# First key and query loads regrouped by queue, first packed queries transposed by halves, one last store, one widening step on GpSimd, and another order

## The chip, the cores and the metric

The kernel runs on one core of a Trainium2 chip. Its time is the device time of one execution in microseconds; the number compared is the median of the runs shown. An engine executes its own instructions in the order in which they were recorded, and waits for other engines and for transfers through semaphores. TensorE is called PE, VectorE DVE, ScalarE ACT, GpSimd POOL and SyncE SP. SP computes nothing here; it issues almost all transfers.

## The reference

Two blocks follow each other: attention through 32 packed queries for each head, then a gated feed-forward block with a convolution of three taps.

```python
# q, k, v: (8, 8, 576, 64) float32, p: (8, 8, 32, 64) float32
def sm_attn(qq, kk, vv):
    s = scale * np.matmul(qq, kk.transpose(0, 1, 3, 2))
    s = s - np.max(s, axis=-1, keepdims=True)
    a = np.exp(s)
    a = a / (np.sum(a, axis=-1, keepdims=True) + 1e-09)
    return np.matmul(a, vv)
p_packed = sm_attn(p, k, v)
out = sm_attn(q, p_packed, p_packed)
x = out.transpose(0, 2, 1, 3).reshape(8, 576, 512)
# w_in (512, 1024), conv_w (3, 1024), w_out (1024, 512): float64
h = np.maximum(x @ w_in, 0.0)
conv_out = sum(conv_w[k] * shifted(h, k - 1) for k in range(3))
gate = 1.0 / (1.0 + np.exp(-conv_out))
return (h * gate @ w_out).astype(np.float32)
```

## The kernel before, in words

The 64 pairs of batch and head are worked through in 16 groups of four heads, `g` = 0 to 15; a batch `b` has two groups. For a group, keys and queries are loaded (`load_kq`) and transposed into `kT` and `qT`: for the first four groups on PE in two halves, five and four blocks of 128 columns (`half_transpose`, L684), which ACT or DVE copy out of PSUM; for the others on DVE (L644). The keys of group 0 come in two transfers of 640 and 512 columns (L606, L608), so that the first five blocks can be transposed ahead of the other four. `attention(g)` then makes the scores of the packed queries `pT` against the keys (L704), the maximum `nm` (L819, DVE), the exponential `a` with its sum (L823, ACT), its transpose (L835) and copy `a1T`, the product with the values (L843), the scaled result `pb` and its transpose `ppT` (L856 to L869), the scores against the queries (L704 again), their softmax on DVE, ACT and POOL (`s`, `mx`, L877 to L907), and the result split into a high and a low part, `a2hi` and `a2lo`.

The packed output is not formed: `packed_weight` multiplies `ppT` into `w_in` (L949, split by L977), and `ffn1(b, j)` (L1014, 12 matmuls for each of 64 pairs of batch and block of 128 columns) multiplies that with `a2`, in three products for the high and low parts. Relu, three taps and a tanh follow on ACT and DVE (L1029 to L1073; L1073 makes the finished block of `hgt`). `ffn2(m)` multiplies 36 tiles of 128 rows with `w_out`: two with plain float32 (L1142), the others with three products of parts (L1195). The last tile is made in two halves of 256 columns (`last_tile`, L1100).

The float64 weights come in as eight tiles of 1 MB. Each is turned to float32 on the core: the upper words by an ACT instruction (L441), the low words by another (`rounding`, L502), a shift on DVE (L445) and an addition on DVE or POOL.

Which engine does a movable step is written in the sets `ON_DVE` and `ON_POOL`. All steps are generators, and the string `ORDER` says in which order they are recorded, two characters for each step. `Flow` goes through it with a table of costs, and before the start of the second tile of `ffn2` it records idle matmuls on zeros (L287, called `warm`) wherever its table has PE waiting for at least one of them; seven matmuls on `stage` (L298) come ahead of everything.

SP issues `p` of the first four groups, queries, keys, values and weights in one fixed sequence. A transfer holds one of eight semaphores, so it waits for the transfer eight places ahead. The keys, queries and weights of the opening lie in `hgt` and `stage`, which are used again.

Of the kernel before, what the change touches and what calls it, by code (L numbers as in the profile page):

```python
# [26 lines left out]
    "140x3j3x3n3z145z0q3z5y5z3x5y3z5y1041143y0x410q0q3p3y3z5z3p7d413y3z0x42153n3p421e42433y443n3p43144238430x605y4344"
    "425y435z5z3p44191d1b1414600w420x5y1b446060435z43453l15421b143l443p45460x44601444456060464546146011464745601b6061"
    "460x45474645465z481b475y17600x0x136049484947611g0x491k141448494847474a4b1i484947184849484961616161621r1i38616162"
    "0x61611i611b381i624b621c0x620x6163141c1b62141n1b0x0x4b1i0x141a62621b6263621f1i14141j1b1p141j624a636363141i1i6363"  # L30
    "1p1p1b1b63646314141p4a1462631i1b391u1b4c4d4c4e4c644d1l1h391b1w1p4c4d4c4d1i634c651p1m641i644e1z1q4d1b644d1q1b1p4e"
    "4c1b1i1i641y1s1p4f641o1w4d1p4e64652164644g1w1i1i1w254f1t1b641x4f651i1x4g4f65644f232c1b4e4k1w4g1p1i4g4e4k4f4e4g1w"
    "65651w4g4k65651b1p1p63664g394h4i651i4f2d4h65664h4j4i231i4i1v65231w4j6666661w664j4h4i4h1p23284i2a23241w4j4h1i4l4l"
    "4j1i1w4j2a4h4j23664i4i66664l6665204m2a4n2a6767241w1p4m4o664n222f1w1p4n2a66674n67672b671p67264n674o4m4n4m67231p1p"
    "4m681w4n4m1p27231p674p234u1w4p2h234m681p674o2b2a4p4o681w2h4p694o684p692h682368292368684p4o4o4q1w23672h4p4q68684u"
    "4q682h1w4q2a4r4r69694s69236a2j4q4q4s4u4q69696a1w234t2a692a692m4r4s694s2o4r4v1w4t4r4t2k694r4s4t2i2a2h4t6a4r4s4s6a"
    "4t4t6a2a6a6a236b2i4v1w6a6a6a6b4w2e4v682o6a2h6b2a4w2o692h6b2g4x4w6b4w6b6b2l2q4x6c6a4y2a234x6b6b2p4x4w4w2o4y4x6b4x"
    "4w236c6b6d2a4x6d4z2x4z232a6c6c2t502h506c2a6c4y504y6c4z6c6c2r502o2a6c6c2p2h23544z2v4y2z2a2h2o4y6c6d6d6d4z236b4z2o"
    "2o6d4z2h506d546d2v6e4y2v2h2h6d6e6d546d5030516e2o50522s6f526e2v53516f2n6e2h2v6e6e2a526e2w532w5151536e6e5352322o51"
    "53522o6e552v536d516f2a2h526f2h512a6f53522h2o6g6f5556322v566f2o566f326f2h6f6g2o6f57586g2u57562o2v6g576g562y582h6g"  # L40
    "5632565759586h6h6e3259556g576g6g2v6g5959573257332v59582o6g595e5e335a6h2o6g59585e5a6h6h6h3258322h5b5a6i2o326h6h5a"
    "6f6h2o5a6i5a585b6h5b5b5a6h5c2o2v2v5b5d6j5b2v315d6i6i6j5d6i2v6i6i5d5c6i2v5d5c6i5d5c2v6i5d6i5f5c5c326j6j6j6j5c5b5f"
    "6j6j6k6i6k6j6j6l2o5f6j5g5h5g6l2v6k326k5g6k6k5i2v6k6k5g2v6k5h5g5g325i5g5i6k5h5h6j6k5j6m6l6l5i5h5i2v6l326l6m5i5j5h"
    "6l325h6l6h5j6l6l5i6l325k5k6m5k5j6n6m5j6m326l5j6m5l5k5j326m6m6m6m2v5m5k5l5k6n6m5l6n5k5n5l5m6m326n325m6n5l5m6n6n6o"
    "5l5n326n6n6o6n5n5o6n5o5m325p6o5p6o5l5m5n5o6o6o6o5n6o6o5p6o5n5n5m6n6p6o5q5r6p5r5q5q5s5r6p6p6p5q6o6p5q5r5q6q5q6p6p"
    "5r6q5s5r6p5s5t5r5s6p5u5t6p5t6q6r5t6q6q6p5s5t6q5u5t6r5u5t6k6q6q5u6q5v5u5s5s6q5u5w5u5v6q5w5x5v6r5x5v6r5x6r6s6s6r6r"
    "5x5w6r5w6r5v6r5x5w5v6s5x5w6s5v5w6s6s5x6s6r6s6t6s6s6r6t6u6t6t6t6t6t6u6t6s6t6q6t6u6t6u6u6u6v6v6u6u6t6u6u6v6u6v6v6w"
    "6s6v6v6v6v6u6v6v6w6w6w6w6x6w6w6w6w6w6x6x6x6v6x6x6x6x6x6w6x7e7e7e7e7e6x7e7e6x7e7e6w7e"
# [15 lines left out]
class Flow:  # L64
# [150 lines left out]
def tile_packed_attention_conv_gate(  # L215
# [1068 lines left out]
```

## Time and profile before

| | |
|---|---|
| median of three runs | 395.87 us (395.81 to 396.06) |
| the profiled execution | 396.32 us, of which the span is 394.5 us |
| PE busy | 386.9 us, 98% of the span |
| DVE, ACT, POOL busy | 336.0 us (85%), 246.1 us (62%), 77.8 us (20%) |
| transfers | 47.63 MB, mean 121 GB/s |

The span is what the profile shows, from the first to the last instruction. Busy shares are means over stages that differ: the transfers are dense in the first third and sparse after it. Matmuls are pipelined, so that neighbouring ones overlap in the profile; the pieces of the chain of waits give their distance instead.

### The profile page before, as it was taken

The numbers are of one execution on the slowest core, as the hardware profiler recorded it, in microseconds if no ns is written. First come the engines' busy times: TensorE is split into PE (matmuls) and PEld (weight loads), VectorE is DVE, ScalarE is ACT, GpSimd is POOL, SyncE is SP. The second block draws the span as 40 slices with busy tenths as digits, with TensorE's granted clock in tenths as the row PEclk, the third lists the DMA queues.
The fourth block names the chain that finished last, engine by engine and source line by source line (L and its number), as shares of the span: only waits on it lengthen the run. The fifth ranks groups of instructions, "written<-read, shape, count | busy, mean of one in ns | idle before, by whom it ended". The sixth has DMA issues, their size and how long they took to land.

```text
span 394.5 us, 8187 instructions
## 1 busy us (share of the span) xinstructions
PE 386.9 (98%) x3306; PEld 310.3 (79%) x3306; DVE 336.0 (85%) x503; ACT 246.1 (62%) x399; POOL 77.8 (20%) x58
## 2 busy tenths in 40 slices
PE   7999999999999999999999999999999999999996
PEld 6657665787778887979788797979798869898885
DVE  4899999999998999999998999899989797967110
ACT  3599999987667777866645545677454433544221
POOL 2042124104234443322002122101010022020020
PEclk9999999999999999999999999999999999999999
DMA  8998898995878995666393461010010000101111
GB/s 263 372 370 258 214 266 147 194 206 97 148 148 165 172 206 112 130 114 139 72 172 68 100 125 50 1 55 2 27 55 24 29 28 28 53 2 53 54 53 56
DMA packets 157543, 47.63 MB, mean 121 GB/s; under 512 B 145460, under 2 KB 148788, under 8 KB 157504
## 3 DMA queue, kind: packets, MB, share of 16 engines
q1 hardware_dynamic: 157104, 46.41, 50.0%
q10 hardware_dynamic: 368, 0.66, 0.6%
q8 instruction: 26, 0.43, 0.5%
q14 instruction: 13, 0.11, 0.1%
q0 software_dynamic: 32, 0.02, 0.0%
HBM read 37.64 MB, written 9.44 MB: 119 GB/s over the span
## 4 chain that ended last, share of the span: by engine, by line
PE 85%; DMA 5%; DVE 3%; ACT 3%; SPq 1%; issue 1%; DVEq 0%; ACTq 0%
PE fo L1195 41%; PE big L1014 23%; PE sm L1195 4%; DMA q<-in_q_dram 4%; PE big L1142 4%; PE big L704 4%; PE big L949 3%; PE sm L843 2%; PE big L835 2%; DMA hgt<-in_q_dram 2%; SPq L623 1%; PE fo L1100 1%; PE sm L1100 1%; PE big L684 1%; ACT hgt L1071 1%
## 5 line engine op out<-in xcount | busy, mean ns | idle before, releaser
L1195 PE MATMUL fo<-wo_hi,xhi 128*128 128x512 f32 x240 | 96.6, 402 | 0.0
L1195 PE MATMUL fo<-wo_lo,xhi 128*128 128x512 f32 x240 | 94.0, 392 | 0.0
L1195 PE MATMUL fo<-wo_hi,xlo 128*128 128x512 f32 x240 | 93.7, 390 | 0.0
L1071 ACT ACTIVATE hgt<-hgt 128x576 f32<-128x576 f32 x64 | 43.6, 688 | 28.8 <-DVE hgt L1067 28.7
L329 POOL TENSOR_TENSOR xlo<-hgt,xhi 128x1024 fp32r<-128x1024 f32 x14 | 35.7, 2548 | 130.4 <-DVE xhi L339 36.0
L1063 DVE SCALAR_TENSOR_TENSOR hgt<-hbuf,cw,hgt 128x576 f32<-128x576 f32 x64 | 53.4, 842 | 9.3 <-ACT hgt L1061 9.1
L1031 ACT ACTIVATE hbuf<-big 128x576 f32<-128x576 f32 x57 | 37.3, 655 | 30.2 <-PE big L1014 30.0
L1014 PE MATMUL big<-a2hi,ghi 128*128 128x288 f32 x256 | 55.8, 299 | 0.0
L1014 PE MATMUL big<-a2lo,ghi 128*128 128x288 f32 x256 | 54.6, 294 | 0.0
L1014 PE MATMUL big<-a2hi,glo 128*128 128x288 f32 x256 | 54.3, 293 | 0.0
L1195 PEld LDWEIGHTS fo<-wo_hi,xhi 128*128 128x128 f32 x240 | 45.1, 188 | 11.5 <-issue 2.2
L1195 PEld LDWEIGHTS fo<-wo_hi,xlo 128*128 128x128 f32 x240 | 45.1, 188 | 10.2
L1195 PEld LDWEIGHTS fo<-wo_lo,xhi 128*128 128x128 f32 x240 | 45.1, 188 | 7.3
L1067 DVE SCALAR_TENSOR_TENSOR hgt<-hbuf,cw,hgt 128x576 f32<-128x576 f32 x64 | 50.6, 808 | 0.2
L1073 DVE SCALAR_TENSOR_TENSOR hgt<-hgt,hbuf 128x576 f32<-128x576 f32 x64 | 48.4, 769 | 2.1 <-ACT hgt L1071 1.6
L1014 PEld LDWEIGHTS big<-a2hi,ghi 128*128 128x128 f32 x256 | 42.7, 188 | 5.5 <-issue 1.6
L1014 PEld LDWEIGHTS big<-a2hi,glo 128*128 128x128 f32 x256 | 40.9, 188 | 0.0
L1014 PEld LDWEIGHTS big<-a2lo,ghi 128*128 128x128 f32 x256 | 40.9, 188 | 0.0
L1210 ACT COPY o<-fo 128x512 f32<-128x512 f32 x30 | 17.6, 585 | 32.8 <-PE fo L1195 28.8
L1061 ACT ACTIVATE hgt<-hbuf,cw 128x576 f32<-128x576 f32 x47 | 36.2, 779 | 2.4 <-DVE hbuf L1029 1.7
L326 DVE TENSOR_TENSOR xlo<-hgt,xhi 128x1024 fp32r<-128x1024 f32 (+1 forms) x24 | 24.6, 1035 | 10.7 <-ACT xhi L341 10.5
L341 ACT CAST xhi<-hgt 128x1024 fp32r<-128x1024 f32 (+1 forms) x28 | 26.8, 957 | 8.8 <-DVE hgt L1073 4.5
(127 smaller groups left out, 576.5 us busy)
## 6 DMA issues: line engine op xcount, KB each, us to landing
out_dram<-o SPq DMA_DIRECT2D x35, 256.0 KB, 2.3
k<-in_k_dram SPq DMA_DIRECT2D x48, 144.0 KB, 3.3
q<-in_q_dram SPq DMA_DIRECT2D x48, 144.0 KB, 3.2
v<-in_v_dram SPq DMA_DIRECT2D x40, 128.0 KB, 3.2
v<-in_v_dram SPq DMA_DIRECT2D x6, 512.0 KB, 7.5
hgt<-in_moe_w_in_dram SPq DMA_DIRECT2D x3, 1024.0 KB, 12.5
hgt<-in_moe_w_out_dram SPq DMA_DIRECT2D x3, 1024.0 KB, 6.2
hgt<-in_q_dram SPq DMA_DIRECT2D x2, 576.0 KB, 6.9
```

The source lines that it names most:

```text
L326: nc.vector.tensor_tensor(**kw)
L329: added = nc.gpsimd.tensor_tensor(**kw)
L341: nc.scalar.copy(out=out, in_=in_)
L1014: nc.tensor.matmul(out=t[:, hf, :SH], lhsT=w[:, gg, js], rhs=x[:, hf * SH : (hf + 1) * SH], start=n == 0, stop=n == (1 if b in F1F else 3) ...
L1031: nc.scalar.activation(out=inner, in_=t[:, :, :SH], func=AF.Relu, scale=0.5)
L1061: nc.scalar.activation(out=d, in_=h[:, 1 : S + 1], func=AF.Copy, scale=cw[:, NJ + j : NJ + j + 1])
L1063: nc.vector.scalar_tensor_tensor(out=d, in0=h[:, 0:S], scalar=cw[:, j : j + 1], in1=d, op0=ALU.mult, op1=ALU.add)
L1067: nc.vector.scalar_tensor_tensor(out=d, in0=h[:, 2 : S + 2], scalar=cw[:, 2 * NJ + j : 2 * NJ + j + 1], in1=d, op0=ALU.mult, op1=ALU.add)
L1071: nc.scalar.activation(out=d, in_=d, func=AF.Tanh)
L1073: nc.vector.scalar_tensor_tensor(out=d, in0=d, scalar=1.0, in1=h[:, 1 : S + 1], op0=ALU.add, op1=ALU.mult)
L1195: nc.tensor.matmul(out=t, lhsT=x[:, c, :], rhs=w[:, c % 2, :], start=c + i == 0, stop=c == NJ - 1 and i == 2)
L1210: nc.scalar.copy(out=o, in_=t)
```

## The change

The first transfers are issued otherwise. On ACT's queue the first 640 columns of the keys of group 0, then its queries in one transfer, then the other 512 columns of the keys; before, the queries came from SP. The values of group 0 get a dependency on the first of these transfers. SP's sequence is another one, given by `ORDER`.

The first packed queries are transposed and scaled by halves: groups 0 and 1, then groups 2 and 3, each half with four transposes and one scaling.

The low words of the first weight tile (`r0`) may be multiplied on POOL, and are. In the opening four copies of `kT`, one of `a1T` and one of `a2hi` go from DVE to ACT and one of `qT` the other way (`kT15`, `kT20`, `kT25`, `kT35`, `a1T0`, `hi0`; `qT05`); more names change later. Costs in the table are changed, which moves idle matmuls: there are 27 instead of 31.

In the last half tile the copy out of PSUM is divided between ACT and DVE, and one store from SP takes the place of two stores of 64 rows from ACT and SP.

```diff
-    "36003602360300360403366y36016y346z34070405053a346z0a0a70340e090505083b700605060c3c050l0c05340h053b0h3e0c72053405"
+    "003603360236360036036y3604070504050a703a05340170053b0e0634340a060936760c080c363b6z3c050c050c050h050c05340l6z0h"
...
-    ON_DVE = {"a1T0", "hi0", "hi1", "hi12", "hi15", "kT10", "kT15", "kT20", "kT25", "kT35", "qT00", "relu35", "relu45", "relu61", "relu66", "relu67", "relu71", "relu74", "tap02", "tap36", "tap42", "tap43", "tap44", "tap46", "tap51", "tap52", "tap61", "tap63", "tap65", "tap66", "tap67", "tap70", "tap72", "tap73", "tap75", "x140", "x170", "x220", "x240", "x250", "x270", "x280", "x300", "x320"}
+    ON_DVE = {"gh510", "hi1", "hi12", "kT10", "qT00", "qT05", "relu34", "relu76", "tap00", "tap02", "tap40", "tap41", "tap42", "tap44", "tap46", "tap53", "tap56", "tap57", "tap60", "tap61", "tap64", "tap65", "tap67", "tap70", "tap72", "tap73", "tap74", "tap75", "tap77", "x140", "x180", "x230", "x270", "x280", "x310", "x340", "x90"}
...
+    def behind(added, old, reason):
+        info = mybir.DependencyInfo(mybir.DependencyClass.Sync, mybir.DependencyReason.DATA)
+        tc.add_manual_dep(added.ins, old.name, info, reason=reason)
...
-        if f"r{i}" in ON_DVE:
+        if key in ON_POOL:
+            old = [x for x in nc.cur_bb.bb.instructions if x.engine == mybir.EngineType.DVE][-2]
+            added = nc.gpsimd.tensor_scalar(out=r, in0=low, scalar1=2.0**-29, scalar2=None, op0=ALU.mult)
+            behind(added, old, "GpSimd waits for its turn beside VectorE")
+        elif key in ON_DVE:
...
+            if g == 0:
+                behind(first, keys[0].ins, "the first keys have the transfer engines to themselves")
...
-                nc.scalar.dma_start(out=t[:, :640], in_=rows[:, :640])
+                keys.append(nc.scalar.dma_start(out=t[:, :640], in_=rows[:, :640]))
...
+            if g == 0:
+                rows = src[b, :HG].rearrange("h (r s) d -> (h r) (s d)", r=NR)
+                nc.scalar.dma_start(out=t, in_=rows)
+                grp[g][name] = t
+                return
...
+            for gs in ((0, 1), (2, 3)):
+                for x in range(2):
+                    for db in range(2):
+                        first, r = x + db == 0, 64 * x + 32 * db
...
+                        nc.vector.transpose(
+                            out=pT[r : r + 32, 128 * gs[0] : 128 * gs[1] + 128].rearrange("d (h n) -> d h n", n=NP),
+                            in_=raw[:, HG * gs[0] : HG * gs[1] + HG, 32 * db : 32 * db + 32],
+                        )
+                yield Step("DVE", 202, two=True, sets=[("pT", g) for g in gs])
+                part = pT[:, 128 * gs[0] : 128 * gs[1] + 128]
+                nc.vector.tensor_scalar(out=part, in0=part, scalar1=SCALE, scalar2=None, op0=ALU.mult)
...
-        nc.scalar.copy(out=o, in_=t)
+        nc.scalar.copy(out=o[:, : DM // 4], in_=t[:, : DM // 4])
+        nc.vector.tensor_copy(out=o[:, DM // 4 :], in_=t[:, DM // 4 :])
         yield Step("SP", 600, give=["o"])
-        nc.scalar.dma_start(out=rows[:64, fs], in_=o[:64])
-        nc.sync.dma_start(out=rows[64:, fs], in_=o[64:])
+        nc.sync.dma_start(out=rows[:, fs], in_=o)
```

At the start of the program ACT issues two transfers before and three after, ahead of its first copies (in these names `hgt_75` is `hgt[0]`, where the first keys and queries lie, and `hgt_76` is `hgt[1]`). Before:

```order
L606 DMA hgt_75<-in_k_dram 128x640
L608 DMA hgt_75<-in_k_dram 128x512
L341 ACT_TABLE_LOAD
L341 COPY kT<-big 128x640
L341 COPY kT<-big 128x512
```

and with the change:

```order
L623 DMA hgt_75<-in_k_dram 128x640
L637 DMA hgt_75<-in_q_dram 128x1152
L625 DMA hgt_75<-in_k_dram 128x512
L345 ACT_TABLE_LOAD
L345 COPY kT<-big 128x640
L345 COPY kT<-big 128x512
```

The queries now stand between the two parts of the keys. SP's sequence at the same place was

```order
L760 DMA stage<-in_p_dram 32x16x64
L623 DMA hgt_75<-in_q_dram 128x1152
L586 DMA v_88<-in_v_dram 128x4x256
L595 DMA v_88<-in_v_dram 64x4x64
L623 DMA hgt_75<-in_k_dram 128x1152
L407 DMA hgt_76<-in_moe_w_in_dram 128x4x512
L623 DMA k<-in_k_dram 128x1152
```

and is now

```order
L783 DMA stage<-in_p_dram 32x16x64
L645 DMA hgt_75<-in_k_dram 128x1152
L411 DMA hgt_76<-in_moe_w_in_dram 128x4x512
L601 DMA v_88<-in_v_dram 128x4x256
L612 DMA v_88<-in_v_dram 64x4x64
L645 DMA k<-in_k_dram 128x1152
L645 DMA hgt_75<-in_q_dram 128x1152
```

The keys of group 1 and the first weight tile moved ahead of the values of group 0, and these two have nothing to wait for. On PE, just ahead of the first `ffn1` product (L1014 before), there stood, from the transposes of the queries of group 2 on,

```order
L684 MATMUL big<-ident,q 128x128 x5
L949 MATMUL big<-w_in_sb,ppT 32x256 x8
L684 MATMUL big<-ident,q 128x128 x4
L843 MATMUL sm<-v_88,a1T 32x64 x20
L835 MATMUL big<-ident,a_483 128x128 x5
L977 MATMUL big<-ghi,minus 128x256 x2
L866 MATMUL sm<-ident,pb 128x128
L287 MATMUL idle<-zeros 128x512 x2
L704 MATMUL big<-qT,ppT 32x288 x8
L287 MATMUL idle<-zeros 128x512
L1014 MATMUL big<-a2hi,ghi 128x288 x2
```

and now stands

```order
L706 MATMUL big<-ident,q 128x128 x5
L977 MATMUL big<-w_in_sb,ppT 32x256 x8
L726 MATMUL big<-kT,pT 32x288 x8
L292 MATMUL idle<-zeros 128x512 x2
L1005 MATMUL big<-ghi,minus 128x256 x2
L706 MATMUL big<-ident,q 128x128 x4
L292 MATMUL idle<-zeros 128x512 x2
L871 MATMUL sm<-v_88,a1T 32x64 x20
L1042 MATMUL big<-a2hi,ghi 128x288 x2
```

A transpose of `a`, a transpose of `pb` and a score against queries moved behind the first product. Of the idle matmuls 25 stood ahead of it and 6 behind; now it is 23 and 4.

## Rows read from the trace of the kernel before

**Rows 1.** Page, busy time, share and instructions by engine.

```profile
PE 386.9 (98%) x3306; PEld 310.3 (79%) x3306; DVE 336.0 (85%) x503; ACT 246.1 (62%) x399; POOL 77.8 (20%) x58
```

**Rows 2.** Windows: stretch, length, busy time by engine, granted clock, DMA share, GB/s.

```profile
0.00:5.00 5.00, 3.87 (x15) 3.42 (x16) 0.71 (x2) 1.28 (x1) 2.07 (x15) 1.00 0.64 186
5.00:10.00 5.00, 3.77 (x38) 2.68 (x38) 4.06 (x7) 2.16 (x5) 0.00 (x0) 1.00 1.06 345
...
46.40:105.00 58.60, 58.52 (x545) 40.93 (x546) 57.82 (x83) 51.88 (x82) 14.65 (x9) 1.00 0.88 174
...
390.60:394.50 3.90, 0.00 (x0) 0.00 (x0) 0.00 (x0) 0.37 (x1) 0.00 (x0) 0.95 0.14 36
```

**Rows 3.** Timeline of PE: start us, us, instruction, idle before it.

```profile
7.20 1.64 PE L684 MATMUL big<-ident,hgt 128*128 128x128 f32 x13 [1.23 <-DMA hgt<-in_q_dram]
...
9.08 0.72 PE L704 MATMUL big<-kT,pT 64*32 64x288 f32 x16
...
33.95 0.42 PE L1014 MATMUL big<-a2hi,ghi 128*128 128x288 f32 x2
...
40.91 1.56 PE L287 MATMUL idle<-zeros 128*128 128x512 f32 x6
...
46.38 0.72 PE L704 MATMUL big<-qT,ppT 64*32 64x288 f32 x16 [0.29 <-ACT ppT L869]
```

**Rows 4.** Transfers issued near 1.2 us: KB, us to landing.

```profile
hgt<-in_q_dram SPq DMA_DIRECT2D x1, 576.0 KB, 6.0
hgt<-in_k_dram ACTq DMA_DIRECT2D x1, 256.0 KB, 6.2
```

**Rows 5.** Transfer queues from 4.5 to 5.5 us: packets, MB, share of 16 engines.

```profile
q1 hardware_dynamic: 55, 0.24, 69.6%
q10 hardware_dynamic: 49, 0.10, 29.6%
```

**Rows 6.** Timeline of ACT and DVE in the opening.

```profile
8.45 0.59 ACT L341 COPY kT<-big 128x512 f32<-128x512 f32 x1 [1.97 <-PE big L684]
...
5.17 2.85 DVE L770 STREAM_TRANSPOSE pT<-stage 32x512 f32<-32x512 f32 x4 [3.58 <-DMA stage<-in_p_dram]
...
9.91 0.76 DVE L819 TENSOR_REDUCE nm<-big 128x1 f32<-128x576 f32 x1 [0.70 <-PE big L704]
11.77 0.82 DVE L339 COPY kT<-big 128x640 f32<-128x640 f32 x1 [1.11 <-PE big L684]
12.64 0.67 DVE L339 COPY kT<-big 128x512 f32<-128x512 f32 x1
...
32.60 0.75 DVE L326 TENSOR_TENSOR a2lo<-a2t,a2hi 128x576 fp32r<-128x576 f32 x1
```

**Rows 7.** Chain that ended last: start us, us, what; pieces for distances.

```profile
7.20 1.22 PE big L684 x9
32.57 0.46 PE idle L287 x2
54.66 0.65 PE big L704 x16
57.22 1.59 PE big L1014 x12
58.81 0.58 PE big L835 x5
```

**Rows 8.** A copy of 128 columns on ACT; the last copy and store; landings of stores.

```profile
16.39 0.26 ACT L869 COPY ppT<-sm 128x128 f32<-128x128 f32 x1
390.68 0.37 ACT L1113 COPY o<-fo 128x256 f32<-128x256 f32 x1 [2.50 <-PE fo L1100]
391.08 0.56 ACTq L1115 DMA_DIRECT2D out_dram<-o  x1
...
out_dram<-o SPq DMA_DIRECT2D x1, 128.0 KB, 1.7
out_dram<-o ACTq DMA_DIRECT2D x1, 64.0 KB, 2.4
```

More of the change, by code (lines that the diff above doesn't have):

```diff
@@ L27 @@
[L27 to L31, printed above, removed]
@@ L329, in tensor_tensor @@
         added = nc.gpsimd.tensor_tensor(**kw)
-        tc.add_manual_dep(
-            added.ins,
-            old.name,
-            mybir.DependencyInfo(mybir.DependencyClass.Sync, mybir.DependencyReason.DATA),
-            reason="GpSimd waits for its turn beside VectorE",
-        )
+        behind(added, old, "GpSimd waits for its turn beside VectorE")
     def copy(key, out, in_):
@@ L496, in rounding @@
     def rounding(i):
-        yield either(f"r{i}", 1048, 1135, two=True, after=[("we", i)], sets=[("wp", i)])
-        low, r = words.pop(i)
-        if f"r{i}" in ON_DVE:
+        key = f"r{i}"
+        on = "GP" if key in ON_POOL else "DVE" if key in ON_DVE else "ACT"
+        ns = dict(ACT=1048, DVE=1135, GP=R_GP)
+        opts = dict(ACT=(1048, False), DVE=(1135, True), GP=(R_GP, 0))
+        yield Step(
+            on, ns[on], either=(key, opts), two=on == "DVE", early=True, after=[("we", i)], sets=[("wp", i)]
+        )
+        low, r = words.pop(i)
+        if key in ON_POOL:
+            old = [x for x in nc.cur_bb.bb.instructions if x.engine == mybir.EngineType.DVE][-2]
+            added = nc.gpsimd.tensor_scalar(out=r, in0=low, scalar1=2.0**-29, scalar2=None, op0=ALU.mult)
+            behind(added, old, "GpSimd waits for its turn beside VectorE")
+        elif key in ON_DVE:
             nc.vector.tensor_scalar(out=r, in0=low, scalar1=2.0**-29, scalar2=None, op0=ALU.mult)
@@ L611, in load_kq @@
             yield Step(
-                "SP", 1450, after=after, late=500 * (g == 0), take=["kq"] * (g >= NG), sets=[(name, g)], parts=parts
+                "SP", 1450 + 450 * (name == "q" and g > 1), after=after, late=300 * (g == 0), take=["kq"] * (g >= NG), sets=[(name, g)], parts=parts
             )
@@ L757, in queries @@
         if i == 0:
-            yield Step("SP", 600, sets=[("p", 0)], late=1000)
+            yield Step("SP", 500, sets=[("p", 0)], late=1000)
             raw = stage[:NP, DFF:].rearrange("n (h d) -> n h d", d=D)
             nc.sync.dma_start(out=raw, in_=p[:2].rearrange("b h n d -> n (b h) d"))
-            plain = max([n + 1 for n in range(4) if n not in QUAD_K], default=1)
-            for x in range(2):
-                for db in range(2):
-                    yield Step(
-                        "DVE", 69 + plain * 133, after=[("p", 0)] * (x + db == 0), take=["pT"] * (x + db == 0), sets=[("pd", 0)] * (x + db == 2)
-                    )
-                    if x + db == 0:
-                        pT = wk.tile([128, 4 * HG * NP], F32, name="pT", tag="pT")
-                    r = 64 * x + 32 * db
-                    nc.vector.transpose(
-                        out=pT[r : r + 32, : plain * 128].rearrange("d (h n) -> d h n", n=NP),
-                        in_=raw[:, : HG * plain, 32 * db : 32 * db + 32],
-                    )
@@ L774, in queries @@
[L774 to L779 removed]
+            pT = None
+            for gs in ((0, 1), (2, 3)):
+                for x in range(2):
+                    for db in range(2):
+                        first, r = x + db == 0, 64 * x + 32 * db
+                        yield Step(
+                            "DVE",
+                            335,
+                            after=[("p", 0)] * first,
+                            take=["pT"] * (first and not gs[0]),
+                            sets=[("pd", 0)] * (x + db == 2 and gs[0] > 0),
+                        )
+                        if pT is None:
+                            pT = wk.tile([128, 4 * HG * NP], F32, name="pT", tag="pT")
+                        nc.vector.transpose(
+                            out=pT[r : r + 32, 128 * gs[0] : 128 * gs[1] + 128].rearrange("d (h n) -> d h n", n=NP),
+                            in_=raw[:, HG * gs[0] : HG * gs[1] + HG, 32 * db : 32 * db + 32],
+                        )
+                yield Step("DVE", 202, two=True, sets=[("pT", g) for g in gs])
+                part = pT[:, 128 * gs[0] : 128 * gs[1] + 128]
+                nc.vector.tensor_scalar(out=part, in0=part, scalar1=SCALE, scalar2=None, op0=ALU.mult)
+                for n in gs:
+                    grp[n]["pT"] = pT[:, 128 * n : 128 * n + 128]
```

76 lines of the change are left out of this document (42 added, 34 removed).

## The prediction

> **What bounds the kernel now.** I read the page's busy times first: PE is busy for 98% of the span, DVE for 85% [rows 1]. Then the windows. From 46.4 to 105 us PE is busy for 58.5 of 58.6 us, and the chain of waits runs on through PE to 390.6 us with no wait of it above 0.3 us. So the middle can hardly give time, only lose some. What is left is the opening, up to 46.4 us, and the 3.9 us behind the last matmul [rows 2]. In the same window DVE is busy for 57.8 of 58.6 us: a second engine stands close behind PE. Third, the timeline of PE in the opening: it waits 1.23 us at 7.20 for keys and queries, has its first score at 9.08, its first product of the feed-forward block at 33.95, and still runs six idle matmuls at 40.91; the score at 46.38 is the last piece that waits noticeably [rows 3]. From 5 to 10 us the transfers move 345 GB/s at a DMA share of 1.06: the opening waits for bytes first, and for DVE and ACT after that [rows 2].
>
> **The opening: bytes.** Before, the second part of the first keys was alone behind the first part on ACT's queue, landing at 7.4 (1.20 + 6.2); the queries, on SP's, at 7.2 (1.20 + 6.0) [rows 4]. Now the queries (0.59 MB) stand ahead of it on ACT's queue, while the keys of group 1 (0.59 MB) and the first weights (1.05 MB) are issued on SP's with nothing to wait for. The new dependency holds back only the values, which come third. How are two queues served together? From 4.5 to 5.5 us, 55 packets of SP's queue (q1) and 49 of ACT's (q10) moved, 0.24 and 0.10 MB: turns about even, and bytes by the size of the packets [rows 5]. Queries and keys of group 1 have rows of one size, and so have the second keys and the weights (2 KB), so I share bytes evenly. Up to the end of the second keys, then, 0.13 (packed queries) + 0.33 + 0.59 + 0.59 + 0.26 + 0.26 (weights) = 2.16 MB must move. By 5 us 0.93 MB are through (186 GB/s), the other 1.23 MB take 3.6 us at 345 GB/s [rows 2], and landings stood about 0.5 us behind such a sum: 9.2 us (an estimate). Its ends are 7.4, as now, if ACT's queue were served first, and 9.8.
>
> The Trainium skill speaks against the change here: the page "DMA: Bandwidth & Descriptors", section "Issuing engines are not separate DMA queues", says that DMAs of SP and ACT run on the same 16 engines and interleave. By it an order within ACT's queue keeps nothing away from what SP has issued, which is the 9.2 of the sum; the plain reading of the change, keys and queries one after the other undisturbed, would give about 7.2.
>
> **The first scores.** At 9.2 PE does the four blocks (about 0.5 us, of the 1.22 us for nine, [rows 7]), ACT copies them (0.59 us, [rows 6]), then comes an idle matmul (0.23 us, [rows 7]) and the score (0.65 us): first score at 10.6, first maximum on DVE at about 11.3 instead of 9.91 [rows 6]. Halving the transposes lets `pT` be ready some 1.6 us earlier (four at 0.71 us become four at about half, [rows 6]). That cover is worthless while the keys are late: DVE then stands idle from about 6.9 to 10.4 us.
>
> **DVE up to the second pair of parts.** The first product needs `a2lo` of group 1. From the first maximum to its end DVE takes 23.4 us now (9.91 to 33.35), of which 1.1 and 0.2 us idle; the 1.11 stands ahead of the copy at 11.77 [rows 6]. In the new order this stretch has three copies of `kT` of 512 columns (about 0.6 us each by their starts), one of 640, one of `a1T` (0.75 each) and one maximum (0.67) less; one copy of `qT` (0.6) and the second half of the packed queries (four at 0.36 and a scaling of 0.24) more [rows 6]. A shift and a high part less and a subtraction more give another 0.3 less. Net about 2.0 us less. The waits: the 1.1 us for the exponential again, and some 0.6 us where scores now come late. 11.3 + 23.4 - 1.3 - 2.0 + 1.7 = 33.1, against 33.35. With the bounds of the landing, 31.3 to 33.8.
>
> What left DVE costs ACT: four copies more and one widening step less (`r0`, on POOL now). For that step on POOL the trace has no row; two-operand instructions of 512 and 1024 columns there take 1.2 to 2.6 us. It must be done by the addition of the first weights, some 3 us after it can start, so I cost it at nothing; without that cover it would be up to 1.5 us late for DVE.
>
> **PE from there.** The first product starts at about 33.2 instead of 33.95, since PE stands ready: 0.7 us gained. But a score (0.65), a transpose (0.58) and a small one (0.1) moved behind it: 1.3 us lost [rows 7]. Between 33.95 and 46.38 lie 12.4 us with about 9.9 us of work (four times 1.59 us for `ffn1`, the rest transposes, values and weights): 2.5 us without work, of which six idle matmuls at 0.23 us make 1.4 [rows 3, 7]. The new order has four there, 0.9 us, and I leave 0.7 us of waits: 1.6 us, so 0.9 gained. The opening comes to -0.7 + 1.3 - 0.9 = **-0.3 us**.
>
> **The end.** Now the copy of 256 columns takes 0.37 us on ACT, and ACT's store of 64 KB lands 2.4 us after its issue. With the change ACT copies 128 columns (0.26 us for that shape) beside DVE, which has nothing to do there; DVE's two copies differ by 0.15 us for 128 columns, so it is no slower. One store of 128 KB from SP landed in 1.7 us [rows 6, 8]. -0.1 - 0.7 = **-0.8 us**; its bounds are -0.1, if the transfer gains nothing, and -0.9.
>
> The page "DMA: Bandwidth & Descriptors", section "Rules for kernel authors", says the same: two transfers to halves of the partitions use the same engines, and one of 128 partitions is better. By it alone the end would gain in the transfer, without a figure.
>
> **The rest.** DVE's instructions over the whole program change by about -1 us (relu to ACT, low parts from POOL back to DVE), ACT's by a few us in an engine that is idle for a third of the span. I cost these at nothing, because PE bounds the middle; if an order has PE waiting once, that is lost in full.
>
> Sum: -0.3 - 0.8 = -1.1 us on an execution of 396.32 us (394.5 of span and 1.8 around it). That execution lies 0.45 us above the median, so I take the 1.1 us off the median: 394.8.
>
> **Rivals.**
>
> *ACT's queue is served first.* The second keys land near 7.4 and everything on DVE and ACT comes 1.8 us earlier: opening -2.1, in all -2.9, 393.0 us. Against it are the even packets [rows 5].
>
> *DVE stays behind, and PE waits for it between 46 and 80 us: slower.* Up to the eighth finished block of `hgt` the order gives DVE as much work as before, within 0.2 us, but some 3 us more idleness in the opening (3.5 + 1.7 now, 0.7 + 1.3 before). DVE has 0.8 us free in 58.6 us [rows 2], so it can't catch up there. If PE has no other work to put ahead, it waits for what DVE lacks: all of it, +3, makes +1.9 with the end, 397.8; half of it +0.4, 396.3. It turns slower by 0.2% from about 1.9 us of such waits. For it: both engines are full in that window. Against it: the order was made anew, and moves some of PE's other work there. Its middle is 397.
>
> *PE's clock falls.* PE would be idle from 6.0 to 9.2 us. The clock is granted in full (2.4 GHz) in every stretch of the trace, but in the 3.9 us after the last matmul its mean is 0.95, so it did fall there [rows 2]. At 1.2 GHz nine transposes, two scores and a transpose (3.1 us) and more would take twice as long, some of it ahead of idle matmuls: about +2.9, in all +1.8, 397.7.
>
> **Chances.** My forecast 0.45 (394.0 to 395.7), ACT first 0.15, DVE behind 0.30, clock 0.10. By 0.2% (0.8 us, about what a measurement here can tell), faster is below 395.1: two thirds of the forecast and all of the first rival with a little of the second, 0.48. Within 0.2%: a third of the forecast and about 0.12 of the second, 0.27. Slower 0.25. Range 392.8 to 397.3: it leaves out half of the clock's case and the upper quarter of DVE's, and a little below. The forecast's own range is 394.0 to 395.7.
>
> **What would show it.** In the profile after, the second keys should land at 9.0 to 9.5, PE's first score start near 10.6, `a2lo` of group 1 end near 33, the first product start near 33.2; PE's end to the span's end should shrink from 3.9 to about 3.1 us. Wrong would be: landing at 7.5 or below, a granted clock below one from 6 to 15 us, or waits of PE of a microsecond between 46 and 105 us.

## Result and the profile after

The changed kernel takes 399.48 us (median of 4, 398.55 to 399.52) against 395.84 us before: a ratio of 1.0088, 95% interval 1.0070 to 1.0105, so about 0.9% slower. The profiled execution took 398.55 us with a span of 396.8 us. It lies 0.93 us below its median, and the profiled one of before lies 0.48 us above its own, so the traces show 2.2 us of the 3.6 us.

The page of the changed kernel, busy time by engine, reads like [rows 1]:

```profile
PE 387.4 (98%) x3302; PEld 311.5 (79%) x3302; DVE 336.3 (85%) x504; ACT 247.5 (62%) x405; POOL 71.6 (18%) x57
```

PE and DVE are busy for 0.5 and 0.3 us more than before, far less than the 2.2 us, so most of the time is a wait. Windows of the changed kernel (stretch, length, busy time by engine, granted clock, DMA share, GB/s) say where it is not, and what is new in the opening:

```profile
46.40:105.00 58.60, 58.25 (x529) 41.65 (x536) 58.25 (x86) 54.10 (x85) 15.66 (x9) 1.00 0.88 167
...
8.00:9.00 1.00, 0.00 (x0) 0.00 (x0) 0.00 (x0) 0.00 (x0) 0.00 (x0) 1.00 1.04 385
...
10.00:11.00 1.00, 1.00 (x13) 0.56 (x19) 0.47 (x1) 0.43 (x1) 0.00 (x0) 0.54 1.08 358
11.00:12.00 1.00, 1.00 (x17) 0.09 (x13) 0.36 (x1) 0.00 (x0) 0.00 (x0) 0.50 1.28 345
...
13.00:14.00 1.00, 1.00 (x8) 0.95 (x7) 0.17 (x2) 0.80 (x2) 0.00 (x0) 0.75 1.01 406
```

From 46.4 to 105 us PE is as full as in [rows 2]. From 8 to 9 us every engine stands idle while the transfers run at 385 GB/s. Then PE works at a granted clock of 0.50, that is at 1.2 GHz, from about 10.1 to 13.5 us; before it was 1.00 there. PE's timeline answers to [rows 3]:

```profile
9.15 1.34 PE L706 MATMUL big<-ident,hgt 128*128 128x128 f32 x9 [2.71 <-DMA hgt<-in_k_dram]
...
10.85 1.21 PE L726 MATMUL big<-kT,pT 64*32 64x288 f32 x16
12.00 1.91 PE L706 MATMUL big<-ident,hgt 128*128 128x128 f32 x9
...
35.17 0.53 PE L1042 MATMUL big<-a2hi,ghi 128*128 128x288 f32 x2
...
48.12 0.72 PE L726 MATMUL big<-qT,ppT 64*32 64x288 f32 x16 [0.32 <-ACT qT L345]
```

PE waits 2.71 us for the second keys, its score takes 1.21 instead of 0.72 us, the first product starts 1.22 us later than before, and the last matmul ends at 393.06 us, 2.45 us later. Behind 10 us no wait of PE is longer than 0.41 us. The landings (KB, us from issue; issued at 1.17, 1.18, 1.71 and 1.70 us) and the share of the queues from 4.5 to 5.5 us answer to [rows 4, 5]:

```profile
hgt<-in_q_dram ACTq DMA_DIRECT2D x1, 576.0 KB, 6.6
hgt<-in_k_dram SPq DMA_DIRECT2D x1, 576.0 KB, 6.3
...
hgt<-in_k_dram ACTq DMA_DIRECT2D x1, 256.0 KB, 7.4
...
hgt<-in_moe_w_in_dram SPq DMA_DIRECT2D x1, 1024.0 KB, 9.0
...
q1 hardware_dynamic: 44, 0.20, 51.6%
q10 hardware_dynamic: 43, 0.20, 50.8%
```

The second keys land at 9.1 us instead of 7.4. The two queues share evenly, packets and bytes. Up to 8.6 us, where ACT's queue has moved its 1.18 MB (keys and queries of group 0), SP's queue (q1) moved about as much (packets, MB, share; the window behind ends in the clock, the DMA share and GB/s):

```profile
q1 hardware_dynamic: 934, 1.26, 41.0%
q10 hardware_dynamic: 431, 1.18, 38.7%
...
5.00:8.60 3.60, 1.44 (x5) 0.72 (x3) 1.47 (x4) 0.69 (x1) 0.00 (x0) 1.00 1.03 385
```

On DVE and POOL ([rows 6]):

```profile
10.53 0.82 DVE L343 COPY qT<-big 128x640 f32<-128x640 f32 x1 [4.00 <-PE big L706]
12.17 0.76 DVE L847 TENSOR_REDUCE nm<-big 128x1 f32<-128x576 f32 x1 [0.82 <-PE big L726]
...
17.20 1.10 DVE L449 TENSOR_SCALAR tmp<-tmp 128x1024 int32<-128x1024 int32 x1
...
34.30 0.76 DVE L335 TENSOR_TENSOR a2lo<-a2t,a2hi 128x576 fp32r<-128x576 f32 x1
...
14.89 2.87 POOL L511 TENSOR_SCALAR tmp<-hgt 128x1024 int32<-128x1024 uint32 x1 [12.21 <-DVE rs L950]
```

DVE stands idle for 4.00 us, its first maximum comes 2.26 us later than before, `a2lo` of group 1 ends at 35.06 instead of 33.35. The low words took GpSimd 2.87 us, and a shift of DVE beside them 1.10 us instead of 0.68. At the end ([rows 8]):

```profile
393.13 0.27 ACT L1141 COPY o<-fo 128x128 f32<-128x128 f32 x1 [2.50 <-PE fo L1128]
...
393.43 0.29 DVE L1142 COPY o<-fo 128x128 f32<-128x128 f32 x1 [15.10 <-ACT o L1141]
...
393.75 0.33 SPq L1144 DMA_DIRECT2D out_dram<-o  x1
...
out_dram<-o SPq DMA_DIRECT2D x1, 128.0 KB, 1.7
```

DVE's copy begins when ACT's has ended, so the two halves take longer than one copy of 0.37 us did.

### The profile page after: what moved, and what is told of

Its sections match the earlier page's. It is cut to its first block, busy times and chain, and to the rows that moved or that the text cites. A ratio compares the mean times of both kernels' runs of the same rounds, so it can differ in the third digit from the quotient of the medians.

```text
span 396.8 us, 8206 instructions
## 1 busy us (share of the span) xinstructions
PE 387.4 (98%) x3302; PEld 311.5 (79%) x3302; DVE 336.3 (85%) x504; ACT 247.5 (62%) x405; POOL 71.6 (18%) x57
## 3 DMA queue, kind: packets, MB, share of 16 engines
q10 hardware_dynamic: 432, 1.18, 0.8%
## 4 chain that ended last, share of the span: by engine, by line
PE 89%; ACT 5%; DMA 2%; DVE 1%; issue 1%; ACTq 0%
PE fo L1223 42%; PE big L1042 24%; PE big L726 4%; PE sm L1223 4%; PE big L1170 4%; PE big L977 4%; PE sm L871 2%; DMA hgt<-in_k_dram 2%; PE big L863 2%; ACT tmp L445 1%; ACT tmp L516 1%; PE big L706 1%; PE fo L1128 1%; PE sm L1128 1%; ACT qT L345 0%
## 5 line engine op out<-in xcount | busy, mean ns | idle before, releaser
L1059 ACT ACTIVATE hbuf<-big 128x576 f32<-128x576 f32 x62 | 40.5, 654 | 53.3 <-PE big L1042 51.9
L1042 PE MATMUL big<-a2hi,ghi 128*128 128x288 f32 x256 | 57.1, 304 | 0.0
L1223 PEld LDWEIGHTS fo<-wo_hi,xlo 128*128 128x128 f32 x240 | 45.1, 188 | 10.1
L1101 DVE SCALAR_TENSOR_TENSOR hgt<-hgt,hbuf 128x576 f32<-128x576 f32 x64 | 47.3, 751 | 3.1 <-ACT hgt L1099 2.7
L338 POOL TENSOR_TENSOR xlo<-hgt,xhi 128x1024 fp32r<-128x1024 f32 x10 | 24.7, 2467 | 91.5 <-ACT xhi L345 58.6
L1089 ACT ACTIVATE hgt<-hbuf,cw 128x576 f32<-128x576 f32 x43 | 33.1, 780 | 2.6 <-DVE hbuf L1057 2.0
L345 ACT CAST xhi<-hgt 128x1024 fp32r<-128x1024 f32 (+1 forms) x29 | 27.6, 957 | 8.5 <-PE fo L1223 4.1
L335 DVE TENSOR_TENSOR xlo<-hgt,xhi 128x1024 fp32r<-128x1024 f32 (+1 forms) x28 | 30.3, 1094 | 0.3
```

The lines of the kernel that those rows point to most:

```text
L335: nc.vector.tensor_tensor(**kw)
L338: added = nc.gpsimd.tensor_tensor(**kw)
L345: nc.scalar.copy(out=out, in_=in_)
L1042: nc.tensor.matmul(out=t[:, hf, :SH], lhsT=w[:, gg, js], rhs=x[:, hf * SH : (hf + 1) * SH], start=n == 0, stop=n == (1 if b in F1F else 3) ...
L1059: nc.scalar.activation(out=inner, in_=t[:, :, :SH], func=AF.Relu, scale=0.5)
L1089: nc.scalar.activation(out=d, in_=h[:, 1 : S + 1], func=AF.Copy, scale=cw[:, NJ + j : NJ + j + 1])
```

## Experiments

Theory A: the second keys come late because the queries ahead of them share the transfers with what SP's queue has issued; PE stands idle, its clock falls, and the delay is passed on. Rival B: GpSimd's step holds DVE back. Rival C: the new order of work is worse by itself. In all experiments with the opening, the numbers of idle matmuls are written out as the kernel compared with had them (27 in the changed kernel, 31 before), so that the planner doesn't move them; nothing else of the order changes. The kernel before ran beside each of them (medians 395.84 to 396.05 us), so that times of different groups of runs can be compared to some 0.2 us.

**Second keys ahead of the queries on ACT's queue.** In the first row of `ORDER` two entries change places:

```diff
-00 36 03 36 02 36 36 00
+00 36 03 36 00 36 36 02
```

> The changed kernel with the second part of the first keys ahead of the queries on ACT's queue; every engine's order stays as in the changed kernel, with its numbers of idle matmuls. Theory A (the late second keys, and the clock that falls while PE is idle for them, cost the 2.4 us that PE lacks at 48 us): the second keys land at 7.0 to 7.8 instead of 9.1, the queries about 9, the first score starts near 9.0 instead of 10.85, the granted clock of 10 to 15 us is above 0.9 instead of 0.66, and the time is 1.5 to 2.5 us below the changed kernel's, about 397. Rival B (the low words of the first weights on GpSimd, 2.87 us, hold DVE back): the landing moves, the first product gains at most 1 us of its 35.17, and the time at most 1 us. Rival C (the new order itself is worse behind the opening): less than 0.5 us.

Measured: 398.41 us, 1.1 below the changed kernel, between what was expected by theory A (1.5 to 2.5) and by rival B (at most 1). Landings, then PE:

```profile
hgt<-in_q_dram ACTq DMA_DIRECT2D x1, 576.0 KB, 7.6
...
hgt<-in_k_dram ACTq DMA_DIRECT2D x1, 256.0 KB, 5.4
```

```profile
9.34 1.33 PE L704 MATMUL big<-ident,hgt 128*128 128x128 f32 x5 [2.03 <-DMA hgt<-in_q_dram]
```

The keys landed at 6.6 us, but now the queries came at 9.3, and the first score at 11.03 us: the expectation for the score was wrong, and so was the one for the clock (0.73 from 10 to 15 us, not above 0.9). Whichever of the two comes last waits for the same bytes, and the first score comes behind both, so this order within ACT's queue gains nothing in the traces (398.76 us against 398.55); the 1.1 us between the medians stays open. Three of the four executions had a mean granted clock of 0.994 to 0.996 over the span (398.36 to 398.76 us); the one with 1.000 took 397.17.

**PE kept busy while it waits.**

```diff
-    IDLE = [0, 2, 0, 1, 0, 0, 2, 1, 0, 1,
+    IDLE = [0, 13, 0, 1, 0, 0, 2, 1, 0, 1,
```

> The changed kernel with 13 instead of 2 idle matmuls ahead of the transposes of the second keys, so that PE is not idle while it waits for them; the keys land as late as before (9.1). Theory A, clock part: the granted clock of 10 to 15 us returns to 0.95 or more, the nine transposes at 12.00 take 1.2 instead of 1.9 us, the score 0.65 instead of 1.21, and the first maximum on DVE comes about 1.0 us earlier; the time falls by 0.8 to 1.5 us, to about 398. If the lateness of the keys alone did it, the clock returns and the time stays within 0.4 us of 399.5. Rivals B and C: no change above 0.4 us.

Measured: 397.69 us (397.59 to 398.11), 1.8 below the changed kernel, somewhat more than expected. PE's timeline:

```profile
5.68 3.46 PE L290 MATMUL idle<-zeros 128*128 128x512 f32 x13
...
10.55 0.71 PE L724 MATMUL big<-kT,pT 64*32 64x288 f32 x16
...
34.39 0.53 PE L1040 MATMUL big<-a2hi,ghi 128*128 128x288 f32 x2
```

The clock is 1.00 in every stretch, the score takes 0.71 us again, the first maximum comes at 11.37, and the first product 0.78 us earlier. So the fallen clock is a part of the loss: 0.8 us between the two traces, 1.8 between the medians. The three executions of the changed kernel that were not profiled had granted clocks of 0.991, 0.996 and 0.991 and took 0.9 us more than the profiled one (0.994), so the mean clock doesn't order these four times, and what the other 1.0 us of the medians is stays open.

**Low words on ACT again.**

```diff
-    ON_POOL = {..., "mul9", "r0", "sub10", ...}
+    ON_POOL = {..., "mul9", "sub10", ...}
```

> The changed kernel with the low words of the first weights on ACT again instead of GpSimd, at the same place of the order. Rival B: DVE's shift and the half copies of pT beside it return from 1.10 to 0.7 us, the subtraction and addition of the first weights come 1 to 2 us earlier, the first product starts 1 to 2 us before 35.17, and the time falls by 1 to 2 us, to 397.5 to 398.5. Theory A: less than 0.5 us, since ACT then has 1 us more of work ahead of its copies while DVE still starts late; it may even lose some. Rival C: less than 0.5 us.

Measured: 398.87 us (398.66 to 401.05), 0.6 below the changed kernel. The profiled execution was the one with 401.05 us: there the second keys landed only at 10.6 us, PE waited 4.52 us for them, and the clock was 0.50 from 10 to 15 us. In this one execution the keys came 1.5 us later than in the changed kernel, and it took 2.1 us more than the next slowest of its four; for GpSimd's price this run says little.

**The same without the fallen clock: 13 idle matmuls and the low words on ACT.** (Both edits above.)

> The changed kernel with 13 idle matmuls ahead of the transposes of the second keys (so the clock stays up) and with the low words of the first weights on ACT again. Beside the run with the idle matmuls alone (397.69) it prices GpSimd's step without the clock in between. If GpSimd's 2.87 us hold DVE back: DVE's shift takes 0.7 instead of 1.37 us, all behind it comes 0.7 us earlier, the first product starts at 33.7 instead of 34.39, the time is 0.5 to 0.9 us lower, about 397.0. If ACT has no room for 1 us more there: the first product does not move or comes later, and the time stays within 0.3 us of 397.7 or rises.

Measured: 397.44 us, 0.25 below the run with the idle matmuls alone (0.4 when each is taken against the kernel before that ran beside it). DVE's shift, and PE:

```profile
16.07 0.69 DVE L447 TENSOR_SCALAR tmp<-tmp 128x1024 int32<-128x1024 int32 x1
```

```profile
16.48 0.71 PE L869 MATMUL sm<-v,a1T 128*32 128x64 f32 x36 [0.96 <-ACT a1T L343]
```

The shift is back at 0.69 us, but ACT with 1 us more work now has PE waiting 0.96 us for a copy; 0.3 us are left at the first product (34.09). Rival B is worth 0.2 to 0.4 us here.

**Queries on SP's queue again, ahead of the keys of group 1.**

```diff
-                nc.scalar.dma_start(out=t, in_=rows)
+                nc.sync.dma_start(out=t, in_=rows)
```

> The changed kernel with the first queries on SP's queue again, second there behind the packed queries and ahead of the keys of group 1; ACT's queue holds only the two parts of the first keys. Every engine's order and the idle matmuls stay. Putting the keys ahead on ACT's queue only moved the lateness to the queries (9.3), so theory A now reads: whichever of the two comes last shares the transfers with what SP has issued, and the first score waits for both. Then here both land near 7.3 (as in the kernel before), the first score starts at 8.8 to 9.3 instead of 10.85, the granted clock stays at 1.00 from 5 to 15 us, the first product starts at 33.3 to 33.8 instead of 35.17, and the time falls by 2.3 to 3.2 us, to about 396.7. If the order behind the opening or GpSimd's low words set the first product, it gains less than 1 us there and the time at most what the idle matmuls gave alone (1.8 us, 397.7).

Measured: 395.52 us (10 executions), ratio to before 0.9993 [0.9984, 1.0003]. Landings, then PE:

```profile
hgt<-in_q_dram SPq DMA_DIRECT2D x1, 576.0 KB, 5.6
...
hgt<-in_k_dram ACTq DMA_DIRECT2D x1, 256.0 KB, 5.9
```

```profile
7.12 1.20 PE L704 MATMUL big<-ident,hgt 128*128 128x128 f32 x9 [0.30 <-DMA hgt<-in_k_dram]
...
8.48 0.72 PE L724 MATMUL big<-kT,pT 64*32 64x288 f32 x16
...
32.31 0.53 PE L1040 MATMUL big<-a2hi,ghi 128*128 128x288 f32 x2
...
45.24 0.72 PE L724 MATMUL big<-qT,ppT 64*32 64x288 f32 x16 [0.30 <-ACT qT L343]
```

This line alone takes back 3.96 us (4.1 against the kernels before that ran beside each), more than the whole loss and more than the 2.3 to 3.2 us expected. Queries and keys land at 6.8 and 7.1 us, the clock stays at 1.00, the first product starts at 32.31. Beside the run with the clock kept up, the first maximum (9.31 against 11.37), the first product and the last score with `qT` (47.29 there) are all earlier by 2.05 to 2.08 us: in the new order the delay of the keys is passed on one for one. Rival C falls in so far as the order is not worse once the keys are on time.

**Keys of group 1 held behind the first keys.** Here the queries stay on ACT's queue.

```diff
+                if g == 1 and name == "k":
+                    behind(one, keys[0].ins, "the first keys have the transfer engines to themselves")
```

> The changed kernel with one dependency more: the keys of group 1 on SP's queue (and by their place in it the first weights behind them) wait, like the values, until the first part of the first keys has landed, at about 4.2 us. Queries and second keys stay one behind the other on ACT's queue, now with the transfers nearly to themselves. If the bytes that SP has issued make the second keys late: up to their end 0.13 + 0.33 + 0.59 + 0.26 = 1.31 MB have to move instead of 2.16, so they land near 6.5 instead of 9.1; first score about 8.1, clock at 1.00, the keys of group 1 land at 8.5 to 9.5 and PE may wait some 0.5 us for them; time 395.0 to 396.0, level with or below the run with the queries on SP (395.52). If the order within ACT's queue itself, or the issue on ACT, makes them late: landing stays above 8.5 and the time above 398.

Measured: 395.77 us, ratio to before 0.9996 [0.9987, 1.0005]. Landings of what ACT issues at 1.17 and 1.71 us, and of the keys of group 1, issued at 4.59 us; then PE:

```profile
hgt<-in_q_dram ACTq DMA_DIRECT2D x1, 576.0 KB, 5.0
...
hgt<-in_k_dram ACTq DMA_DIRECT2D x1, 256.0 KB, 5.1
...
hgt<-in_k_dram SPq DMA_DIRECT2D x1, 576.0 KB, 4.8
```

```profile
9.51 1.17 PE L706 MATMUL big<-ident,hgt 128*128 128x128 f32 x9 [0.54 <-DMA hgt<-in_k_dram]
```

The second keys land at 6.8 us with the queries ahead of them on the same queue. So the queue is not what makes them late; the bytes on SP's queue are. What is pushed back is missed next: PE waits 0.54 us for the keys of group 1.

**The same with the low words on ACT.** (Both edits.)

> The run before with the low words of the first weights on ACT again. By the pair with the idle matmuls, 0.25 us below the run before: 394.8 to 395.7. If the earlier scores find ACT full: no gain, and PE's wait for a copy on ACT grows beyond 1 us.

Measured: 395.89 us, ratio 0.9999 [0.9986, 1.0011]: no gain. PE's wait for the copy of `a1T` on ACT is 1.58 us, as the second branch had it. With GpSimd's step taken away, then, the time fell by 0.25 to 0.4 us with late keys, and it rose by 0.1 here.

**The kernel before with the queries between the keys on ACT's queue.**

```diff
-                nc.sync.dma_start(out=t, in_=rows.rearrange("h r f -> (h r) f"))
+                on = nc.scalar if g == 0 else nc.sync
+                on.dma_start(out=t, in_=rows.rearrange("h r f -> (h r) f"))
```

> The kernel before with one thing of the change: the first queries go out on ACT's queue between the two parts of the first keys, so that the values, the keys of group 1 and the first weights move up on SP's queue. Its order of work and its idle matmuls stay. Theory A: the second keys land near 9 instead of 7.4, PE waits 2 to 3 us there, the granted clock falls below 0.8 in the 3 us behind it, the first maximum on DVE comes at 11.5 to 12.2 instead of 9.91, and the time rises by 1.5 to 3 us, to 397.3 to 398.8. If the new order of work were the cause, the time stays within 0.6 us of 395.8.

Measured: 396.69 us, ratio 1.0023 [1.0010, 1.0036]: slower, but by 0.7 to 0.9 us, less than expected. The profiled execution (397.88 us) had queries at 7.9 and keys at 8.8 us; PE, and the window behind:

```profile
7.92 3.04 PE L683 MATMUL big<-ident,hgt 128*128 128x128 f32 x13 [2.26 <-DMA hgt<-in_q_dram]
```

```profile
8.00:9.00 1.00, 1.00 (x5) 0.99 (x6) 0.24 (x1) 0.00 (x0) 0.00 (x0) 0.50 0.94 323
```

Thirteen transposes took 3.04 us instead of 1.64. By the mean clocks (0.994 and 0.996, 398.54 and 397.88 us) such a fall is in two of the ten executions; of the other eight, seven took 396.27 to 396.76 and one 397.55. So in the old order the late bytes cost about 0.6 us, and 1.2 to 2 more where the clock falls. The same move of the queries costs 4 us in the new order. In the old one PE has five transposes of queries ahead of those of the second keys: they began 0.72 us later than before (7.92 against 7.20), and the keys landed while they ran. In the new order the second keys' transposes stand first, and PE stands idle until 9.15. SP's sequence differs between the two as well, so that this pair doesn't separate the two orders cleanly.

**The new end alone, in the kernel before.**

```diff
-        nc.scalar.copy(out=o, in_=t)
+        nc.scalar.copy(out=o[:, : DM // 4], in_=t[:, : DM // 4])
+        nc.vector.tensor_copy(out=o[:, DM // 4 :], in_=t[:, DM // 4 :])
...
-        nc.scalar.dma_start(out=rows[:64, fs], in_=o[:64])
-        nc.sync.dma_start(out=rows[64:, fs], in_=o[64:])
+        nc.sync.dma_start(out=rows[:, fs], in_=o)
```

> The kernel before with the changed end of the last half alone: ACT and DVE copy 128 columns each, and one store of 128 KB goes out from SP. My prediction gave this -0.8 us. Theory now, from the trace of the changed kernel, where DVE's copy began only when ACT's had ended: 0.27 and 0.29 us one after the other are 0.2 us longer than the one copy of 0.37, and the store gains at most 0.7 us; PE's end to the span's end shrinks by 0.1 to 0.3 us and the time by as much, which hardly shows. If the two copies run side by side here, the gain is 0.6 to 0.8 us.

Measured: 395.47 us, ratio 0.9990 [0.9981, 0.9999]. The last copy, and the window from PE's end:

```profile
390.78 0.29 DVE L1114 COPY o<-fo 128x128 f32<-128x128 f32 x1 [14.14 <-ACT o L1113]
```

```profile
390.41:393.80 3.39, 0.00 (x0) 0.00 (x0) 0.29 (x1) 0.27 (x1) 0.00 (x0) 1.00 0.12 41
```

PE's end to the span's end is 3.39 instead of 3.89 us. From PE's end to the issue of the store it is 0.69 us, against 0.48 with one copy [rows 8]: the copies cost 0.2 us and the store gains 0.7. The two copies run one after the other, as expected, but the gain (0.5 us at the end, 0.4 in the time) is more than the 0.1 to 0.3 expected.

**One copy and one store, in the kernel before.** (The store's edit alone.)

> The kernel before with the last half copied by ACT alone, as before, and stored by one DMA of 128 KB from SP. Theory (the two copies of the change run one after the other and give back 0.2 us, the single store gains 0.5 to 0.7): PE's end to the span's end shrinks from 3.9 to 3.2 to 3.4 us and the time by 0.4 to 0.7 us, to about 395.3, some 0.2 us better than with the two copies (395.47). If the store gains nothing: 395.8.

Measured: 395.50 us, ratio 0.9987 [0.9978, 0.9996]; PE's end to the span's end 3.31 us. Both forms of the end gain 0.4 to 0.5 us; one copy is not measurably better than two.

**Queries on SP's queue and low words on ACT, in the changed kernel.**

> The changed kernel with the first queries on SP's queue again and the low words of the first weights on ACT: only the halves of the packs, the new end and the new order are left of the change. With the keys late, taking GpSimd's step away gave 0.25 us (397.69 to 397.44), less than the 0.7 us by which it had stretched DVE's shift, because PE then waited 0.96 us for a copy on ACT. If that holds with early keys too: 395.52 - 0.25, about 395.3. If ACT is fuller there: 395.5 or above. If GpSimd's step was what ate the gain of the halves: 394.8.

Measured: 395.39 us (11 executions), ratio 0.9988 [0.9979, 0.9997], 0.1 below the run with the queries' edit alone, as the first branch had it. It beats both kernels, but the kernel before does as well with nothing but the new end or the new store (395.47 and 395.50).

**Queries on SP's queue and the old end, in the changed kernel.**

> The changed kernel with the first queries on SP's queue again and the end of the kernel before (one copy on ACT, two stores of 64 KB): what is left of the change are the halves of the packs, GpSimd's step, the changed lists of engines and the new order. If the new end is all that this version (395.52 with the new end) has over the kernel before, the time rises by 0.4 to 0.5 us to about 396.0 and is the same as before. If the new order gains in the opening as well (PE ended 0.4 us earlier in that profile), it stays at 395.5 to 395.7.

Measured: 397.00 us, ratio 1.0027 [1.0014, 1.0039], slower than before. The median stands for no execution: six of twelve took 395.94 to 396.43, the profiled one among them, and six 397.57 to 398.12, four of these with a clock of 0.996. Those with the lower time answer to the first branch (about 396.0); why half of them took 1.6 us more stays open, since none of those has a profile. With the queries on SP's queue and the new end there were one of ten (397.19) and one of eleven (396.93) such times, and four in the 71 of the kernel before in these groups (397.29 to 397.50). That the halves, the new lists and the new order cost nothing with early keys is therefore shown for the usual executions, and not for all. None of the three was run by itself.

## Why the prediction was wrong

The forecast was 394.8 us, the range 392.8 to 397.3; 399.48 lies above both.

*The bytes: the mechanism right, the number in part by luck.* The keys landed at 9.1 us against 9.2, and the queues shared evenly; holding SP's transfers back confirms the cause. But the sum's terms 5 + 3.6 + 0.5 make 9.1, not 9.2, and two of them were off against each other: 2.46 MB had moved by 8.6 us where I had 2.16 (by my own even share SP's queue had to move 1.18, not 0.98), and they moved at 385 GB/s from 5 to 8.6 us where I had 345.

*PE's clock: the step that failed first.* I forecast the first scores at full clock and put the fall down as a rival with 0.10, although I had PE idle from 6.0 to 9.2 us. PE waited 2.71 us and the clock went to 0.50. With the clock up, the first score started at 10.55 and the first maximum came at 11.37, where I had 10.6 and 11.3: the rest of that step holds. The rival's price of 2.9 us in the opening was too high: 0.8 us in the traces, 1.8 in the medians. I had doubled the work, but nine transposes took 1.91 instead of 1.20 us and the score 1.21 instead of 0.72. Its total of 397.7 is, by coincidence, what the kernel took with the clock up. That this lies above the range too shows that the clock was not all.

*DVE's stretch: mis-sized.* From the first maximum to the end of `a2lo` I had 21.8 us (11.3 to 33.1). It took 22.89 us in the changed kernel, with the clock up (11.37 to 34.26) and with early keys (9.31 to 32.20): 1.1 us more. Windows of this stretch, before and changed (length, then busy time of PE, PEld, DVE, ACT, POOL):

```profile
9.91:33.35 23.44, 22.68 (x342) 14.65 (x342) 21.58 (x43) 18.98 (x37) 4.89 (x4) 1.00 1.00 338
...
12.17:35.06 22.89, 21.79 (x323) 15.05 (x323) 20.48 (x42) 18.91 (x37) 5.32 (x3) 0.97 1.05 372
```

DVE is busy for 1.1 us less (0.85 with early keys, 20.73), where I had 2.0 less; its idle time grew by 0.3 to 0.55 us, where I had 0.4. So the work was mis-sized and the waits were about right. The shift beside GpSimd's step is 0.4 to 0.7 us of what is missing. "Costed at nothing" for that step was wrong by its length (2.87 us, above my bounds of 1.2 to 2.6) and near in the time (0.25 us).

*PE behind the first product: mis-sized.* I had 1.3 us more work there and 0.9 fewer idle matmuls and waits, net +0.4. From the product's delay to that of PE's end the traces give +1.2 (2.45 - 1.22), and with early keys again +1.2 (-0.43 at PE's end, -1.64 at the product). Windows of PE from the first product to its end, before and changed, separate the two terms:

```profile
33.95:390.61 356.66, 356.06 (x2913) 289.29 (x2911) 309.60 (x452) 222.74 (x357) 70.34 (x39) 1.00 0.48 104
...
35.17:393.06 357.89, 357.09 (x2939) 290.27 (x2932) 311.85 (x454) 225.63 (x365) 64.15 (x39) 1.00 0.52 98
```

Before, PE waited for 0.60 us there and ran six idle matmuls (1.4 us): 2.0, not the 2.5 I had taken. Now it waits for 0.80 and runs four (0.9): 1.7, near my 1.6. So the gain there was 0.3 instead of 0.9, and the work that moved there cost about 1.5 instead of 1.3.

So the opening was +2.45 us in the trace, not -0.3: 0.8 for the clock, 1.1 for DVE, 0.8 behind the product. The step that failed as a whole is the claim that DVE's shorter list pays for keys that are 1.7 us late. The list is shorter by 0.55 us (22.89 against 23.44), not by 1.6, and a first score 2 us late is 2 us at the end.

*The end: -0.4 to -0.5, not -0.8.* The store gained 0.7 us as said; the copy lost 0.2 instead of gaining 0.1. In the profile of the changed kernel only 0.2 us of it is seen (3.7 against 3.9), since the span ended about 1.3 us after the landing instead of 1.0; why, no run shows.

*The rivals.* ACT's queue served first: no, the packets are even. DVE behind: DVE is late by its idleness in the opening, but it shows as PE's delay before 48 us, and the longest wait of PE between 46 and 105 us is 0.32 us. With early keys all edits but the queue come to nothing beside the new end: with the queries on SP's queue the changed kernel takes 395.52, the kernel before with the new end 395.47, each 0.4 to 0.5 below the kernel before that ran beside it.

In the medians: 3.96 us for the queue in this order, of which 1.8 went when PE was kept busy in the wait (0.8 in the traces) and 2.2 are the delay itself; -0.3 to -0.5 for all the rest, the end included.

## What to carry to other kernels

Count the bytes that are issued on all queues up to the landing that the first instruction waits for; a transfer moved to another queue gives its old place to whatever stood behind it. A load that starts the longest chain of the opening cost its delay one for one here (2.06 us at the first maximum, 2.17 at the end), and less where PE had other loads to work on first, as in the old order. And where TensorE must wait, price the work behind the wait at the lower clock too (1.6 to 1.9 times as long here), or give it idle matmuls.

## What the runs showed of the hardware

Granted clock: PE idle for 2.71 us, behind two idle matmuls, was followed by 0.50 (1.2 GHz) in the changed kernel, and the clock also fell with waits of 2.03, 2.26 and 4.52 us in three other profiles; 0.66 us in the same place with SP's transfers held was not followed by a fall, nor 1.23 us in the kernel before.

GpSimd and DVE: in five profiles DVE's shift (128x1024, int32) began under GpSimd's step of 2.87 to 2.90 us and ended 0.54 to 0.56 us after that step's end, whenever it had begun, in 1.10 to 1.39 us instead of 0.69; transposes beside it kept their 0.43 us. The Trainium skill, page "SBUF — State Buffer", section "Who interferes with whom", calls the port pair that the two engines share an exclusive lock, and says that VectorE's `tensor_scalar` can take it in its two-port modes; the shift is such an instruction. Five profiles are as with such a lock, though none shows the mode. In the sixth, with the keys of group 1 held, the shift ran in 0.69 us inside GpSimd's step, and the instruction behind it was held instead:

```profile
12.37 3.19 POOL L509 TENSOR_SCALAR tmp<-hgt 128x1024 int32<-128x1024 uint32 x1 [9.70 <-DMA hgt<-in_moe_w_in_dram]
...
13.98 0.69 DVE L447 TENSOR_SCALAR tmp<-tmp 128x1024 int32<-128x1024 int32 x1
14.59 1.05 DVE L365 TENSOR_SCALAR s<-s 24x128 int32<-24x128 int32 x1
```

That instruction takes 0.20 us in the other five; here it took 1.05 and ended 0.08 us after GpSimd's step.

Two copies out of one tile: DVE's began only when ACT's had ended, in every profile with the new end. The Trainium skill, page "PSUM — Partial Sum Buffer", section "PSUM bank collisions raise a hardware error", says that the compiler puts a dependency between two engines that touch one bank and quadrant, reads included; the trace agrees (0.27 and 0.29 us one after the other, DVE released by ACT's copy). Both copies also write one tile, `o`, so that no run shows which of the two tiles made the dependency.
